# A reordered first attention stage with a contiguous mask and more filler matmuls, in a fused retention and gated MLP kernel

## The chip, the cores and the metric

The kernel runs on one core of a Trainium2 chip. The metric is the device time of one execution in microseconds (us). The time before is the median of four runs, 319.27 us (318.81 to 320.63). One of the runs was taken with the hardware profiler; its views are what this text reads.

The engines are named as in the profile: PE is the matrix engine (PEld its weight loads), DVE the vector engine, ACT the scalar engine, POOL the general-purpose engine; SP only issues DMAs here. A "q" behind a name (SPq, ACTq) is the engine's queue issuing a DMA. Each engine works through its own instructions in order and waits on semaphores for the others.

## What is computed

Eight batches, eight heads, 576 positions, head dimension 64. Attention with a decay in place of a softmax, then a gated MLP on the joined heads:

```python
scores = scale * np.matmul(q, k.transpose(0, 1, 3, 2))
gamma = 1.0 - 2.0 ** (-5.0 - np.arange(H))
Dmat = np.where(rel >= 0, gamma[:, None, None] ** rel, 0.0)   # rel = row - column
ret = np.matmul(scores * Dmat, v)                              # (B, H, S, D)
x = ret.transpose(0, 2, 1, 3).reshape(B * S, H * D)            # 4608 x 512
h = x @ w_in                                                   # 512 -> 2048
g = h * (1.0 / (1.0 + np.exp(-beta * h)))
out = g @ w_out                                                # 2048 -> 512
```

All inputs and the output are float32; the kernel works in bfloat16 with float32 accumulation.

## The kernel before

The decay is split into a gain on q (gq) and one on v (gv), so that the scores need only a 0/1 causal mask. Of each batch the first 512 positions are taken as four chunks of 128; the last 64 positions of two batches share a tail chunk. A chunk passes through these steps, each a small function:

- `pre_q`, `pre`: scale q by gq (for batch 0 on DVE), cast k to kn and scale v to vn (on POOL).
- `t_q`, `t_k` (L283, L290): transpose q and k on PE into PSUM; ACT copies the result to kT (L294), and ACT and DVE one half of qT each (L288).
- `a_sc` (L303): eight score matmuls (L311) into two PSUM tiles of 128x512, one for each half of the heads. DVE multiplies each with the mask into R (L321). The mask is one 128x128 tile, broadcast over four heads. For chunk 3 of batch 0 (`i == CB - 1`), the second PSUM tile is first copied by ACT to an SBUF tile, `half` (L318).
- `a_st` (L369): four matmuls of kn and vn (L379) that add this chunk to a running state; ACT copies it out twice, 64 partitions each (L384), to `sbd` or, for the last chunk, `end`.
- `a_cross` (L323): four matmuls of the state before this chunk with qT (L340). Chunk 0 has none.
- `a_O` (L345 to 367): eight matmuls of R and vn (L354); the sum is copied to xT, the MLP's input, by ACT (L367), and for chunk 3 by DVE and ACT, one half each (L364, L365).

The MLP of a block of 512 rows is `up` (L389: sixteen hidden blocks of four 512-column matmuls each, L396, and a Silu on ACT, L398) and `down` (L402: L409, a copy by DVE, a store issued by SP). Weights come as float32 pieces: w_in in two pieces of 256 columns and three of 512, w_out in four. They are cast by `cast_w_in` (L174) and `cast_w_out` (L186). In `cast_w_in` the first two pieces go mostly to POOL: of piece 0 only `ko == 0` is DVE's.

The order of the work is written out by hand. The first stage, batch 0's attention, is the list of calls at L440 to L477. From L484 on, batch n's MLP on PE is the "fill", and the steps of later batches (transposes, scores, state, outputs, loads) are merged into it at given positions. Loads are issued by SP in program order: q of batch 0, k and v of its four chunks, five pieces of w_in, then w_out's four, q of batch 1, k and v of its chunks, q of batch 2 and so on. Several wait until a staging buffer is free.

`warm_up(n, cols)` (L198) issues n float32 matmuls on zeros, whose result nobody reads. Here they are called filler. The profile shows each as two instructions. `betas_safe` (L209) makes four small DVE operations on the 2048 betas; Silu and the w_out casts read what it leaves.

Of the kernel before, what the change touches and what calls it, by code (L numbers as in the profile page):

```python
# [12 lines left out]
BF16 = mybir.dt.bfloat16  # L13
ACT = mybir.ActivationFunctionType
ALU = mybir.AluOpType
# [4 lines left out]
def kernel(  # L20
# [10 lines left out]
    nc = tc.nc  # L31
# [4 lines left out]
    P = 128  # L36
    HP = H // 2
# [3 lines left out]
    CB = MB // P  # L41
# [16 lines left out]
    consts = ctx.enter_context(tc.tile_pool(name="consts", bufs=1))  # L58
# [67 lines left out]
    for h in range(H):  # L126
# [12 lines left out]
    causal = consts.tile([P, P], BF16, name="causal")  # L139
    nc.gpsimd.memset(causal[:], 1.0)  # L140
    nc.gpsimd.affine_select(out=causal[:], in_=causal[:], pattern=[[1, CB], [CB, PC]], compare_op=ALU.is_ge,
                            fill=0.0, base=0, channel_multiplier=-1)

    causal2 = consts.tile([P, P], BF16, name="causal2")

# [28 lines left out]
    def cast_w_in(g, kos=range(KO)):  # L174
        t = wts[g]
        f0, fn = pieces[g]
        for ko in kos:
            on_pool = ko == KO - 1 or g == 0 and ko > 0 or g == 1 and ko > 1
            (nc.gpsimd if on_pool else nc.vector).tensor_copy(w_in_sb[:, ko, f0:f0 + fn], t[:, ko])  # L179
# [18 lines left out]
    def warm_up(n, cols=256):  # L198
        ph = psum.tile([P, MB], F32, name="ph", tag="mm", bufs=3)
        for _ in range(n):  # L200
            nc.tensor.matmul(ph[:, :cols], warm[:, :P], warm[:, :cols], start=True, stop=True,  # L201
                             skip_group_check=True)
# [6 lines left out]
    def betas_safe():  # L209

        nc.vector.tensor_tensor(tiny[:], beta_sb[:], beta_sb[:], ALU.mult)
        nc.vector.tensor_scalar(tiny[:], tiny[:], 1e-24, 1e-12, ALU.is_lt, ALU.mult)
        nc.vector.tensor_tensor(beta_sb[:], beta_sb[:], tiny[:], ALU.add)
        nc.vector.reciprocal(rbeta_sb[:], beta_sb[:])
# [5 lines left out]
    def xt(m):  # L220
        if m not in xts:
            xts[m] = xpool.tile([P, HP, CB, P], BF16, name="xT", tag="xT" if m < B else "xTt", bufs=3 if m < B else 1)
        return xts[m]
# [4 lines left out]
    def gains(g, c):  # L228
        return g[:, c, :].unsqueeze(2).to_broadcast([P, H, D])
# [15 lines left out]
    def pre(i):  # L245

        b, c = seq[i]
        vn = sb.tile([P, H, D], BF16, name="vn", tag="vn", bufs=5)
        if b is None:
            t = tail_tiles.pop(c)  # L250
            qk = sb.tile([P, 2, H, D], BF16, name="kn", tag="kn", bufs=3)
            qkT = sb.tile([P, 2, HP, P], BF16, name="kT", tag="kT", bufs=3)
            nc.gpsimd.tensor_tensor(qk[:, 0], t[:, 0], gains(gq, CB), ALU.mult)
            nc.gpsimd.tensor_copy(qk[:, 1], t[:, 1])
            nc.gpsimd.tensor_tensor(vn[:], t[:, 2], gains(gv, CB), ALU.mult)
            live[i] = dict(qk=qk, qkT=qkT, kT=qkT[:, 1], vn=vn)
            return
        if c % 2 == 0:
            pair[b, c // 2] = (sb.tile([P, 2, H, D], BF16, name="kn", tag="kn", bufs=3),
                               sb.tile([P, 2, HP, P], BF16, name="kT", tag="kT", bufs=3))  # L260
        t = kv_tiles.pop(i)
        kn, kT = pair[b, c // 2]
        live[i] = dict(kn=kn[:, c % 2], kT=kT[:, c % 2], vn=vn)
        nc.gpsimd.tensor_copy(kn[:, c % 2], t[:, 0])  # L264
        nc.gpsimd.tensor_tensor(vn[:], t[:, 1], gains(gv, c), ALU.mult)  # L265

    def heads(t, p):
        return t[:, 2 * p:2 * p + 2, :].rearrange("p h d -> p (h d)")
# [14 lines left out]
    def t_q(b, u):  # L283
        T = psum.tile([P, CB, 2, P], BF16, name="T", tag="T" if u == 0 else "mm", bufs=1 if u == 0 else 3)
        for i in range(CB):
            for p in range(2):
                nc.tensor.transpose(T[:, i, p, :], heads(batch[b]["qs"][:, i], 2 * u + p), ident[:])
        (nc.vector.tensor_copy if u else nc.scalar.copy)(batch[b]["qT"][:, :, 2 * u:2 * u + 2], T[:])  # L288

    def t_k(i):  # L290
        T = psum.tile([P, HP, P], BF16, name="T", tag="T", bufs=1)
        for p in range(HP):
            nc.tensor.transpose(T[:, p, :], heads(live[i]["kn"], p), ident[:])  # L293
        nc.scalar.copy(live[i]["kT"], T[:])  # L294

    def q_cols(i, r, p):

        b, c = seq[i]
        if b is None:
            return live[i]["qkT"][r, 0, p, :], lambda o: o  # L300
        return (batch[b]["qT"][r, :, p, c * PC:(c + 1) * PC], lambda o: o.rearrange("k (i s) -> k i s", i=CB))

    def a_sc(i):  # L303
        L = live[i]
        L["R"] = R = sb.tile([P, 2, HP, P], BF16, name="R", tag="R", bufs=2)
        sc = [psum.tile([P, HP, P], F32, name="sc", tag="sc", bufs=2) for _ in range(2)]
        for p in range(HP):
            for j in range(2):
                r = slice(j * D, (j + 1) * D)
                rhs, view = q_cols(i, r, p)  # L310
                nc.tensor.matmul(view(sc[j][:, p, :]), L["kT"][r, p, :], rhs, start=True, stop=True,  # L311
                                 skip_group_check=True)
        mask = causal if seq[i][0] is not None else causal2
        m_b = mask[:].unsqueeze(1).to_broadcast([P, HP, P])
        if i == CB - 1:

            half = sb.tile([P, HP, P], BF16, name="half", tag="half", bufs=1)
            nc.scalar.copy(half[:], sc[1][:])  # L318
            sc[1] = half
        for j in range(2):  # L320
            nc.vector.tensor_tensor(R[:, j], sc[j][:], m_b, ALU.mult)  # L321

    def a_cross(i, first):  # L323

# [18 lines left out]
    def a_O(i):  # L343

        b, c = seq[i]  # L345
        L = live[i]

        early = i < E
        if not early:
            L["O"] = psum.tile([P, HP, P], F32, name="O", tag="O", bufs=1)  # L350
        O, R, vn = L["O"], L["R"], L["vn"]
        crossed = b is None or c > 0
        for j, p in [(n // HP, n % HP) if early else (n % 2, n // 2) for n in range(H)]:
            nc.tensor.matmul(O[j * D:(j + 1) * D, p, :], vn[:, 2 * p + j, :], R[:, j, p, :],  # L354
                             start=p == 0 and not (early and crossed), stop=early or not crossed,
                             skip_group_check=True)
        if not early:
            a_cross(i, False)
        if b is None:
            x = xt(B)[:, :, c, :]  # L360
        else:
            x, O = xt(b)[:, :, :, c * PC:(c + 1) * PC], O.rearrange("k p (i s) -> k p i s", i=CB)
        if i == CB - 1:
            nc.vector.tensor_copy(x[:, :2], O[:, :2])  # L364
            nc.scalar.copy(x[:, 2:], O[:, 2:])  # L365
        else:
            (nc.scalar.copy if i < E else nc.vector.tensor_copy)(x, O[:])  # L367

    def a_st(i):  # L369

        b, c = seq[i]
        if b is None:
            return
        L = live[i]
        if c == 0:
            state_ps[b] = psum.tile([P, HP, P], F32, name="st", tag="st", bufs=1)
        st = state_ps[b]
        for p in range(HP):
            nc.tensor.matmul(st[:, p, :], heads(L["kn"], p), heads(L["vn"], p),  # L379
                             start=(c == 0 and p == 0), stop=True, skip_group_check=True)  # L380
        s = ends[b % 4] if c == CB - 1 else sbds[c % NS]
        for j in range(2):
            r = slice(j * D, (j + 1) * D)
            nc.scalar.copy(s[r, :, j * D:(j + 1) * D], st[r, :, j * D:(j + 1) * D])  # L384
# [57 lines left out]
    for n in range(4):  # L442
        pre_q(0, n)
    t_q(0, 0)
    t_q(0, 1)
    pre(0)
    t_k(0)
    a_sc(0)
    betas_safe()
    a_st(0)  # L450
    pre(1)
    t_k(1)
# [1 line left out]
    a_cross(0, True)  # L454
    a_O(0)
    a_sc(1)
    pre(2)
    a_cross(1, True)
    t_k(2)
    a_st(1)  # L460
    a_sc(2)
    pre(3)
    a_O(1)
    warm_up(1, 128)
    a_cross(2, True)
    t_k(3)
    a_st(2)
    cast_w_in(0, range(1, KO))
    a_sc(3)
    a_O(2)  # L470
    a_cross(3, True)
    a_st(3)
    warm_up(1, 128)
    cast_w_in(0, range(1))
    warm_up(1, 128)
    a_O(3)
    cast_w_in(1)  # L477

# [107 lines left out]
```

## Time and profile before

| what | value |
|---|---|
| median of four runs | 319.27 us (318.81 to 320.63) |
| the profiled execution, device time | 319.38 us |
| its span in the profile | 317.6 us |
| PE busy | 304.8 us (96%) |
| PEld / DVE / ACT / POOL busy | 155.2 / 109.0 / 142.1 / 96.7 us |
| mean granted PE clock | 0.988 of full |
| DMA moved, over the span | 52.79 MB, mean 166 GB/s |
| PE idle, longest single wait after 20 us | 1.64 us, for kT at 78.58 us |

So 1.8 us of the device time lie around the span. Row 2 of the profile page cuts the span in 40 slices of 7.9 us and gives busy tenths for each engine, the PE clock that was granted, and the DMA engines' share; one slice stands out in the clock, the second, at 5 tenths. A busy PE is no proof that PE is the bound in a stage, so the views by window, the timeline and the chain of waits are read as well. In the timeline a line has start, length, engine, source line, operation, output and inputs, shapes and count; brackets give the idle time just before and who ended it.

### The profile page before, as it was taken

What the parts mean: (1) busy time and instruction counts of PE and PEld (TensorE: products, weight loads), DVE (VectorE), ACT (ScalarE), POOL (GpSimd) and SP (SyncE); (2) the same over time, 40 slices, a digit from 0 to 9 for tenths busy, and PEclk for the clock granted to TensorE, in tenths of its full rate; (3) what the DMA queues carried; (4) which work ended last, traced back from release to release, by engine and by line L of the source; (5) the groups of instructions that cost most, each with busy time, mean ns of one, the idle gap of its engine ahead of it and who ended that gap; (6) DMA issues with size and microseconds to landing.
All of it is one profiled execution on the core that took longest, in us unless ns stands there. A gap on an engine that the chain in (4) does not pass through costs nothing.

```text
span 317.6 us, 5273 instructions
## 1 busy us (share of the span) xinstructions
PE 304.8 (96%) x2111; PEld 155.2 (49%) x2147; DVE 109.0 (34%) x193; ACT 142.1 (45%) x246; POOL 96.7 (30%) x127
## 2 busy tenths in 40 slices
PE   7889999997999999999999999999999999999994
PEld 5554455644554445444445444444454444444444
DVE  6655474123560235223323443233333320010012
ACT  5477636873228600770167215730474028207600
POOL 2752075928401932084362300833300000000000
PEclk9599999999999999999999999999999999999999
DMA  7999999999939994999999617997701110031011
GB/s 201 222 372 386 376 224 271 229 279 190 203 100 217 193 203 126 206 196 212 225 251 165 132 68 217 200 188 193 166 0 35 66 68 0 12 88 35 0 66 68
DMA packets 123368, 52.79 MB, mean 166 GB/s; under 512 B 105664, under 2 KB 115280, under 8 KB 123344
## 3 DMA queue, kind: packets, MB, share of 16 engines
q1 hardware_dynamic: 97968, 46.15, 60.6%
q10 hardware_dynamic: 25376, 6.30, 12.6%
q8 instruction: 17, 0.28, 0.4%
q14 instruction: 7, 0.06, 0.1%
HBM read 36.71 MB, written 9.44 MB: 145 GB/s over the span
## 4 chain that ended last, share of the span: by engine, by line
PE 73%; SPq 11%; DMA 8%; POOL 2%; issue 2%; DVE 1%; ACT 0%; ACTq 0%; POOLq 0%
PE po L409 33%; PE ph L396 30%; SPq L92 8%; DMA qn<-in_q_dram 4%; DMA wt<-in_moe_w_in_dram 4%; PE O L354 3%; PE sc L311 3%; PE O L340 2%; PE st L379 2%; POOL qs L241 2%; SPq L81 2%; SPq L171 1%; SPq L419 1%; DVE w_in_sb L179 0%; PE O L337 0%
## 5 line engine op out<-in xcount | busy, mean ns | idle before, releaser
L396 PE MATMUL ph<-xT,w_in_sb 128*128 128x512 bf16 (+2 forms) x575 | 127.6, 373 | 2.1 <-DVE xT L364 0.5
L409 PE MATMUL po<-w_out_sb,gT 128*128 128x512 bf16 (+2 forms) x589 | 126.8, 367 | 0.9
L398 ACT ACTIVATE gT<-ph,beta_sb 128x512 bf16<-128x512 f32 (+2 forms) x148 | 99.1, 676 | 62.7 <-PE ph L396 56.5
L396 PEld LDWEIGHTS <-w_in_sb 128*128 128x128 bf16 x592 | 56.1, 98 | 64.8 <-issue 0.9
L409 PEld LDWEIGHTS <-gT 128*128 128x128 bf16 x608 | 57.2, 98 | 61.4 <-ACT gT L398 0.3
L321 DVE TENSOR_TENSOR R<-sc,causal 128x512 bf16<-128x512 f32 x71 | 45.6, 683 | 68.7 <-PE sc L311 68.7
L416 DVE COPY ot<-po 128x512 f32<-128x512 f32 (+2 forms) x38 | 25.2, 663 | 113.8 <-PE po L409 111.2
L241 POOL TENSOR_TENSOR qs<-qn,gq 128x512 bf16<-128x512 f32 x26 | 27.5, 1082 | 64.6 <-DMA qn<-in_q_dram 64.6
L265 POOL TENSOR_TENSOR vn<-kvn,gv 128x512 bf16<-128x512 f32 x32 | 33.4, 1044 | 26.6 <-PE st L379 13.2
L384 ACT CAST sbd<-st 64x256 bf16<-64x256 f32 x48 | 17.6, 366 | 41.7 <-PE st L379 31.0
L264 POOL CAST kn<-kvn 128x512 bf16<-128x512 f32 x32 | 19.6, 611 | 28.4 <-DMA kT<-kn 11.5
L384 ACT CAST end<-st 64x256 bf16<-64x256 f32 x16 | 5.9, 366 | 37.4 <-PE st L379 37.4
L367 DVE CAST xT<-O 128x512 bf16<-128x512 f32 x28 | 19.1, 680 | 0.9 <-PE O L337 0.9
L311 PEld LDWEIGHTS <-kT 64*128 64x128 bf16 x288 | 8.5, 97 | 16.7 <-issue 11.0
L311 PE MATMUL sc<-qT,kT 64*128 64x128 bf16 x256 | 13.5, 226 | 3.2 <-ACT kT L294 3.0
L354 PE MATMUL O<-R,vn 128*64 128x128 bf16 x288 | 15.4, 230 | 0.0
L379 PE MATMUL st<-vn,kn 128*128 128x128 bf16 x128 | 12.9, 225 | 0.1
L354 PEld LDWEIGHTS <-vn 128*64 128x64 bf16 x288 | 9.5, 112 | 4.3 <-issue 0.8
L340 PE MATMUL O<-qT,sbd 128*128 128x128 bf16 x96 | 9.7, 225 | 0.0
L379 PEld LDWEIGHTS <-kn 128*128 128x128 bf16 x128 | 8.8, 100 | 1.6 <-issue 0.2
L294 ACT COPY kT<-T 128x512 bf16<-128x512 bf16 x12 | 7.0, 586 | 4.5 <-PE T L293 3.7
L201 PE MATMUL ph<-warm 128*128 128x256 f32 (+1 forms) x18 | 6.6, 516 | 1.3 <-DVE warm L114 1.3
(55 smaller groups left out, 86.3 us busy)
## 6 DMA issues: line engine op xcount, KB each, us to landing
qn<-in_q_dram SPq DMA_DIRECT2D x16, 512.0 KB, 5.7
kvn<-in_k_dram SPq DMA_DIRECT2D x32, 256.0 KB, 5.5
kvn<-in_v_dram SPq DMA_DIRECT2D x32, 256.0 KB, 5.5
out_dram<-ot SPq DMA_DIRECT2D x31, 256.0 KB, 2.8
wt<-in_moe_w_out_dram SPq DMA_DIRECT2D x4, 1024.0 KB, 9.2
wt<-in_moe_w_in_dram SPq DMA_DIRECT2D x3, 1024.0 KB, 11.0
out_dram<-ot SPq DMA_DIRECT2D x9, 128.0 KB, 2.4
wt<-in_moe_w_in_dram SPq DMA_DIRECT2D x2, 512.0 KB, 5.4
```

The lines of the kernel that those rows point to most:

```text
L92: nc.sync.dma_start(t[:, j], src[b, :, c * P:(c + 1) * P, :].rearrange("h s d -> s h d"))
L241: e.tensor_tensor(batch[b]["qs"][:, cs, hs], q_tiles[b][:, hs, cs].rearrange("p h i d -> p i h d"), gq[:, cs, hs].unsqueeze(3).to_broadcas ...
L265: nc.gpsimd.tensor_tensor(vn[:], t[:, 1], gains(gv, c), ALU.mult)
L311: nc.tensor.matmul(view(sc[j][:, p, :]), L["kT"][r, p, :], rhs, start=True, stop=True, skip_group_check=True)
L321: nc.vector.tensor_tensor(R[:, j], sc[j][:], m_b, ALU.mult)
L354: nc.tensor.matmul(O[j * D:(j + 1) * D, p, :], vn[:, 2 * p + j, :], R[:, j, p, :], start=p == 0 and not (early and crossed), stop=early or ...
L379: nc.tensor.matmul(st[:, p, :], heads(L["kn"], p), heads(L["vn"], p), start=(c == 0 and p == 0), stop=True, skip_group_check=True)
L384: nc.scalar.copy(s[r, :, j * D:(j + 1) * D], st[r, :, j * D:(j + 1) * D])
L396: nc.tensor.matmul(ph, w_in_sb[:, ko, fo * P:(fo + 1) * P], xts[m][:, ko, :, w], start=(ko == 0), stop=(ko == KO - 1))
L398: nc.scalar.activation(gts[m][:, fo, :, w], ph, ACT.Silu, scale=beta_sb[:, fo:fo + 1])
L409: nc.tensor.matmul(po[:, :nn], gT[:, fo, ms, :], w_out_sb[:, fo, n0:n0 + nn], start=(fo == 0), stop=(fo == FO - 1))
L416: nc.vector.tensor_copy(ot, po[:, :nn])
```

## The change

Five things are edited, all in the first stage:

1. A second mask tile, `causal4`, 128 x 4 x 128, is made on POOL by a copy of the mask with a broadcast; the two maskings of chunk 3 of batch 0 read it instead of the broadcast view.
2. `t_k(3)` goes from behind `a_cross(2)` to ahead of `a_O(1)`; `a_sc(3)` from behind the casts of w_in's piece 0 to ahead of them.
3. `betas_safe()` goes from behind `a_sc(0)` to behind `a_sc(1)`.
4. Filler calls of 128 columns: one more between the two q transposes, two more ahead of `a_sc(0)`, one fewer behind `a_O(1)`.
5. The two single fillers on either side of the last cast of piece 0 become one call of two ahead of it.

```diff
+    causal4 = consts.tile([P, HP, P], BF16, name="causal4")
+    nc.gpsimd.tensor_copy(causal4[:], causal[:].unsqueeze(1).to_broadcast([P, HP, P]))
...
-            nc.vector.tensor_tensor(R[:, j], sc[j][:], m_b, ALU.mult)
+            nc.vector.tensor_tensor(R[:, j], sc[j][:], causal4[:] if i == CB - 1 else m_b, ALU.mult)
...
     t_q(0, 0)
+    warm_up(1, 128)
     t_q(0, 1)
     pre(0)
     t_k(0)
+    warm_up(2, 128)
     a_sc(0)
-    betas_safe()
     a_st(0)
     pre(1)
     t_k(1)
...
     a_O(0)
     a_sc(1)
+    betas_safe()
     pre(2)
     a_cross(1, True)
     t_k(2)
     a_st(1)
     a_sc(2)
     pre(3)
+    t_k(3)
     a_O(1)
-    warm_up(1, 128)
     a_cross(2, True)
-    t_k(3)
     a_st(2)
+    a_sc(3)
     cast_w_in(0, range(1, KO))
-    a_sc(3)
     a_O(2)
     a_cross(3, True)
     a_st(3)
-    warm_up(1, 128)
+    warm_up(2, 128)
     cast_w_in(0, range(1))
-    warm_up(1, 128)
     a_O(3)
     cast_w_in(1)
```

## The prediction

> **What bounds the kernel now.** The change touches only the first stage (batch 0's attention, up to about 20 us of a span of 317.6 us), so the question is what the rest of the kernel waits for. I read three views: the windows (one row per stretch: start:end, length, busy time of PE, PEld, DVE, ACT, POOL with instruction counts, granted PE clock, DMA share, GB/s), the timeline, and the chain of waits.
>
> The first stage, one row per microsecond:
>
> ```profile
> 8.00:9.00 1.00, 0.77 (x8) 0.45 (x8) 0.51 (x2) 0.03 (x1) 0.57 (x1) 1.00 1.37 214
> 9.00:10.00 1.00, 0.32 (x7) 0.30 (x8) 0.24 (x1) 0.59 (x1) 0.72 (x1) 0.68 1.37 218
> ...
> 15.00:16.00 1.00, 1.00 (x16) 0.68 (x16) 0.42 (x1) 0.51 (x2) 0.67 (x2) 0.50 1.13 267
> 16.00:17.00 1.00, 1.00 (x17) 0.94 (x14) 0.87 (x2) 0.59 (x1) 0.66 (x1) 0.91 1.04 336
> ```
>
> The granted clock drops to 0.50 at about 9.3 us and returns to 1.00 at about 16.1, the only dip before the last slices. All the while the DMA share stays at or above 1: loads are back to back.
>
> Next, the seam between the stage and the batch-0 up-projection, in the timeline:
>
> ```profile
> 20.41 3.84 PE L396 MATMUL ph<-xT,w_in_sb 128*128 128x512 bf16 x16 [0.54 <-DVE xT L364]
> 23.20 1.51 DVE L179 CAST w_in_sb<-wt 128x512 bf16<-128x512 f32 x3 [2.36 <-DMA wt<-in_moe_w_in_dram]
> 24.43 0.10 PEld L396 LDWEIGHTS <-w_in_sb 128*128 128x128 bf16 x1 [0.65 <-DVE w_in_sb L179]
> 24.77 0.76 PEld L396 LDWEIGHTS <-w_in_sb 128*128 128x128 bf16 x5 [0.24 <-DVE w_in_sb L179]
> ```
>
> PE starts the up-projection at 20.41 us, does the four hidden blocks of w_in's first 512 columns, and then stands at the second 512. They are cast by DVE from 23.20 on; DVE had been idle 2.36 us, waiting for their DMA. Weight loads at 24.43 and 24.77 wait for those casts. This is **gate 1**: whatever PE has done before, the second load can't go before 24.4, nor the third before 24.8. After it PE runs without a gap to 34.7.
>
> Then the chain that ended last, in order of time (start, length, who):
>
> ```profile
> 15.46 13.14 DMA wt<-in_moe_w_in_dram
> 28.62 1.52 DVE w_in_sb L179 x3
> ...
> 48.90 5.76 DMA qn<-in_q_dram
> ...
> 64.63 7.56 DMA qn<-in_q_dram
> ...
> 77.94 0.59 ACT kT L294
> 78.58 0.40 PE sc L311 x8
> ```
>
> PE enters this chain only at 78.58 us. Before that it is loads, SP's issues of them, and POOL's scaling of what landed. The timeline shows the end of this stretch:
>
> ```profile
> 72.35 4.05 POOL L241 TENSOR_TENSOR qs<-qn,gq 128x512 bf16<-128x512 f32 x4 [4.72 <-DMA qn<-in_q_dram]
> 76.43 1.47 ACTq L271 DMA_TRANSPOSE qT<-qs  x1
> 77.94 0.59 ACT L294 COPY kT<-T 128x512 bf16<-128x512 bf16 x1 [0.80 <-issue]
> 78.58 0.23 PEld L311 LDWEIGHTS <-kT 64*128 64x128 bf16 x8 [1.94 <-ACT kT L294]
> 78.58 0.40 PE L311 MATMUL sc<-qT,kT 64*128 64x128 bf16 x8 [1.64 <-ACT kT L294]
> ```
>
> The q load lands at 72.35, POOL scales until 76.40, ACT's transpose DMA stands in front of its kT copy, and PE sits idle for 1.64 us. This is **gate 2**. The first stage can move the end only by getting through both.
>
> **The change part by part.** The compiled queues show which moves are real. SP's order is the same, so no load moves. PE gets two more 128-column filler calls in all; the transpose of chunk 3 (t_k(3)) goes ahead of a_O(1) and of the cross matmuls of chunk 2; DVE's four beta operations go from ahead of chunk 1's masking to behind it; ACT's kT copy of chunk 3 goes ahead of its xT copy of chunk 1; POOL gets one copy. Moving a_sc(3) ahead of the casts changes no queue's order: those casts are POOL's.
>
> *Fillers.* Two calls follow each other at 18.85 and 19.13: 0.28 us each at full clock. The new one between t_q(0,0) and t_q(0,1) lies where PE is idle 0.53 us for qs at 7.51: free. The two ahead of a_sc(0) take 2 x 0.28 = 0.56 where PE is idle 0.68 us for kT at 9.71: free at full clock. Without that cover, at the half clock, they take 1.12 and make a_sc(0) 0.44 late. The one taken out behind a_O(1) saves up to 0.37 (16.05 to 16.42). The last two are only put together: 0.
>
> Will the clock stay up? The dip begins after a stretch from 6 to 9.3 us in which PE's row is busy about two thirds; 0.84 us more makes it about nine tenths. Every matmul between 9.7 and 16.1 is paid double (eight score matmuls 0.61 against 0.40), so if the clock holds, PE has up to half of those 6.4 us, 3.2, more room there. I take it at even odds. [...]
>
> *Chunk 3's scores.* kn of chunk 3 is ready at 15.80 (POOL 15.19 + 0.61, held by its load); today t_k(3) starts at 16.65. Moved up, it starts at about 15.86, and PE now waits there for POOL. Behind this wait stand a_O(1), chunk 2's cross, a_st(2) and a_sc(3); of these ACT's xT copy of chunk 1 pays, since ACT has to do it after kT instead of before. ACT then goes: kT from about 16.25, 0.59; xT, 0.59; the two state copies, 0.76; half from about 18.1, 0.59, to 18.7. Today half ends at 18.92. So chunk 3's last R is ready 0.2 to 0.3 us earlier, and so is the up-projection: about 20.1 instead of 20.41. Bounds: if ACT's queue did not hold half, the whole 0.8 of t_k(3) and the filler would come through, about 1.0 earlier; with the clock still falling and 0.44 late at a_sc(0), 0.4 later. I take 0.3 earlier, nearest to ACT's rows.
>
> *Betas.* The four operations run from 11.62 to 13.71 and hold chunk 1's masking until 13.62, while its scores were done at about 13.3: 0.3 us off that wait. What is late next is chunk 2's masking: betas from about 13.7 take 0.9 if POOL is not in the way and 2.0 as now. The 1.04 of the first, on 16 columns, lies beside a POOL vn of 11.59 to 12.63, and the next vn is at 14.02 to 15.06. So it begins between 14.9 and 15.7, against 15.58: between 0.7 earlier and 0.1 later, with a_O(2) behind it, not the last thing late. I take 0. Their readers are far off (ACT's first at 21.48).
>
> *Mask.* The copy on POOL, 128x512, is like the kn casts, 0.61; POOL is idle 4.94 us until 7.96: free. Bounds for it: 0.3 (the select of 128 columns) to 1.1 (a two-input 512). If it held DVE's memsets (to 4.40), there are 0.83 us before DVE's next. The gain: the R from half took 0.43 with the broadcast mask, the one from PSUM 0.69. [...] By the rows alone the gain lies between 0 and 2 x 0.26 (as if both fell by the step between them); I take 0, as R from half is already at the lower row.
>
> **The sum.** Stage one: 0.3 earlier (bounds 1.0 or, with the mask's upper bound, 1.5 earlier; 0.4 later). At gate 1 all of "earlier" is lost: PE waits at w_in's second piece instead, and "later" is free up to 0.6 us: the fifth block's third matmul can't start before its load is done (24.77 + 0.10 = 24.87), and PE on its own would reach it after 18 matmuls of 0.214 (10.27 us from 24.44 to 34.71, less the 0.2 of that wait, over 47), at 20.41 + 3.85 = 24.26. Left: 0. Gate 2 would take another 1.64. So 319.38 us for the profiled execution stays 319.4; its median over runs is 319.27, 0.1 lower, so I predict **319.3 us**. Runs spread from 318.81 to 320.63; about half of that, 0.9, is what I allow for on either side.
>
> **Rivals.**
> 1. *No change, with the clock still dipping* (the fillers do not do what they are for). PE at 11 to 16 us stays doubled, the stage ends up to 0.4 late, inside gate 1's 0.6. 319.3 again. For it: PE's idle time there is mostly replaced, not removed. Together with my forecast, 0.91.
> 2. *The dip falls later, on the up-projection: slower.* A faster first stage waits more for the same loads; if the clock then falls at about 20 us and takes as long as today's 6.8 us to return, PE loses 3.4 us. Less gate 1's 0.6 that is 2.8; less gate 2's 1.64, 1.2 us: 320.5. If the delay reaches POOL and SP as well and gate 2 moves with it, the whole 2.8: 322.1. It decides from a loss of 2.2 us on (0.6 + 1.64). Against it: the up-projection's PE row is dense from 20.4. 0.05.
> 3. *The gates are softer than they look: faster.* If the w_in pieces landed earlier and gate 2 followed, the 1.0 to 1.5 us would show: 317.8 to 318.3, at most with a little of the 1.64 too, 317. Against it: DMA share 1.04 from 20 to 40 us, and an unchanged SP queue. 0.04.
>
> **How the numbers follow.** 0.5% (1.6 us) is about what a measurement of this kernel can tell from no change. Faster by more than that: 0.03, a part of rival 3. Slower: 0.04, a part of rival 2. Same: 0.93. The range takes in the forecast, rival 1 and the spread between runs, and the start of rivals 2 and 3: 318.4 to 320.3.
>
> **What would show it.** In the profile after: the clock's row at 9 to 16 us, held or not; the first up matmul between 19.0 and 20.8; DVE's casts of w_in at 23.2 as now, with a longer PE wait for them at 24.4; the score matmuls of gate 2 still at about 78.6 behind kT, idle about 1.6. I am wrong if those two times move, or if a clock dip appears after 20 us.

## The result, and the profile after

The changed kernel takes 318.89 us (median of 53 runs, 317.58 to 321.65); beside it the kernel before took 319.38 (median of 79, 317.79 to 322.97). The ratio is 0.9988, with a 95% interval of 0.9976 to 1.0000: 0.12% less, and an interval that reaches up to no change: no change by the bound of the prediction. The profiled execution took 318.56 us, its span is 316.8; before, 319.38 and 317.6. Of the 0.8 us between the spans only 0.05 are work: DVE's last copy of an output begins at 313.51 instead of 313.56. The rest lies in how long the last stores took: from the start of that copy to the end of the span 4.0 us before, 3.3 after.

So the stage did change, and the end did not. The windows of the changed kernel (columns as before):

```profile
8.00:9.00 1.00, 0.72 (x9) 0.55 (x10) 0.51 (x2) 0.07 (x1) 0.62 (x1) 1.00 1.35 217
9.00:10.00 1.00, 0.82 (x14) 0.60 (x12) 0.28 (x1) 0.59 (x1) 0.70 (x1) 1.00 1.36 221
...
15.00:16.00 1.00, 0.11 (x2) 0.11 (x3) 0.93 (x4) 0.14 (x1) 0.69 (x2) 1.00 1.13 268
16.00:17.00 1.00, 1.00 (x20) 0.81 (x19) 0.74 (x2) 0.67 (x2) 0.65 (x1) 1.00 1.09 351
```

The granted clock, third from the right, stays at 1.00. PE's busy share from 15 to 16 us falls from 1.00 to 0.11: the matmuls at a clock of 0.50 are gone, and what they leave is idle time.

The timeline of the changed kernel, at gate 1 and then at gate 2 (source lines are two higher than before):

```profile
20.15 3.98 PE L398 MATMUL ph<-xT,w_in_sb 128*128 128x512 bf16 x16 [0.52 <-DVE xT L366]
23.27 1.51 DVE L181 CAST w_in_sb<-wt 128x512 bf16<-128x512 f32 x3 [2.70 <-DMA wt<-in_moe_w_in_dram]
24.49 0.10 PEld L398 LDWEIGHTS <-w_in_sb 128*128 128x128 bf16 x1 [0.65 <-DVE w_in_sb L181]
24.83 1.19 PEld L398 LDWEIGHTS <-w_in_sb 128*128 128x128 bf16 x7 [0.24 <-DVE w_in_sb L181]
...
72.45 4.05 POOL L243 TENSOR_TENSOR qs<-qn,gq 128x512 bf16<-128x512 f32 x4 [5.06 <-DMA qn<-in_q_dram]
76.53 1.33 ACTq L273 DMA_TRANSPOSE qT<-qs  x1
77.89 0.59 ACT L296 COPY kT<-T 128x512 bf16<-128x512 bf16 x1 [0.66 <-issue]
78.53 0.40 PE L313 MATMUL sc<-qT,kT 64*128 64x128 bf16 x8 [1.50 <-ACT kT L296]
```

The up-projection starts at 20.15 us instead of 20.41. The casts it then waits for start at 23.27, 0.07 later than before, and the loads of weights behind them at 24.49 and 24.83, 0.06 later. The 0.26 us are gone at gate 1. Gate 2 is where it was.

The chain of waits of the changed kernel is the old one, piece by piece:

```profile
15.50 13.17 DMA wt<-in_moe_w_in_dram
28.70 1.52 DVE w_in_sb L181 x3
...
48.98 5.97 DMA qn<-in_q_dram
...
64.73 7.56 DMA qn<-in_q_dram
...
77.89 0.59 ACT kT L296
78.53 0.40 PE sc L313 x8
```

### The profile page after: what moved, and what is told of

Read it like the earlier page. It is cut to its first block, busy times and chain, and to the rows that moved or that the text cites. A ratio compares the mean times of both kernels' runs of the same rounds, so it can differ in the third digit from the quotient of the medians.

```text
span 316.8 us, 5283 instructions
## 1 busy us (share of the span) xinstructions
PE 302.7 (96%) x2115; PEld 153.8 (49%) x2151; DVE 108.4 (34%) x193; ACT 141.9 (45%) x246; POOL 97.0 (31%) x128
## 4 chain that ended last, share of the span: by engine, by line
PE 74%; SPq 11%; DMA 8%; POOL 3%; issue 2%; DVE 1%; ACT 0%; ACTq 0%; POOLq 0%
PE po L411 34%; PE ph L398 30%; SPq L92 8%; DMA qn<-in_q_dram 4%; DMA wt<-in_moe_w_in_dram 4%; PE O L356 3%; PE sc L313 3%; POOL qs L243 2%; PE O L342 2%; PE st L381 2%; SPq L81 2%; SPq L173 1%; SPq L421 1%; DVE w_in_sb L181 0%; PE O L339 0%
## 5 line engine op out<-in xcount | busy, mean ns | idle before, releaser
L266 POOL CAST kn<-kvn 128x512 bf16<-128x512 f32 x32 | 19.6, 612 | 27.6 <-DMA kT<-kn 11.3
L203 PE MATMUL ph<-warm 128*128 128x128 f32 (+1 forms) x22 | 6.1, 416 | 1.3 <-DVE warm L114 1.3
```

## The experiments

All ratios are to the kernel before, run on the same chip in the same job, with 95% intervals. The kernel before read medians of 319.5, 320.6 and 319.9 us in the three jobs, so kernels of different jobs are compared by ratio.

### The fillers alone, and the moved steps alone

The first kernel is the one before with edits 4 and 5, the second with edits 2 and 3.

```diff
 fillers alone
     t_q(0, 0)
+    warm_up(1, 128)
     t_q(0, 1)
...
     t_k(0)
+    warm_up(2, 128)
     a_sc(0)
...
     a_O(1)
-    warm_up(1, 128)
...
-    warm_up(1, 128)
+    warm_up(2, 128)
     cast_w_in(0, range(1))
-    warm_up(1, 128)
```

> The kernel before with the fillers of the change alone (edits 4 and 5). Theory of the two gates: the clock holds at 1.00 from 9 to 16 us as in the changed kernel, since the fillers are what holds it; the up-projection's first matmul starts at 20.2 to 20.6 us (t_k(3) is still behind the cross matmuls); PE waits for w_in's second 512 columns until 24.4 to 24.9 and for kT until 78.5; the time is within 0.3 us of both kernels, ratio 0.998 to 1.001. Rival, the clock is held by the new order and not by the fillers: a dip to 0.5 between 9 and 16 us remains. Rival, the stage passes through to the end: the time moves by as much as the first up matmul.

> The kernel before with the moved steps alone (edits 2 and 3: t_k(3), a_sc(3), the betas), its old fillers and the old mask. Theory of the two gates: the dip to 0.5 between 9 and 16 us is there as before; chunk 3's half is ready 0.1 to 0.4 us earlier than in the kernel before (18.9) because ACT's queue holds it; first up matmul 20.1 to 20.5 us; the waits at 24.4 to 24.9 and 78.5 stay; ratio 0.998 to 1.002. Rival, the order is what gains the 0.1 per cent that was measured: ratio like the changed kernel's, 0.9988, and no part of it in the fillers alone.

Measured: fillers alone 0.9987 (0.9947 to 1.0027), median 318.93; moved steps alone 1.0001 (0.9971 to 1.0032), median 319.2. The timeline of the fillers alone:

```profile
15.82 0.40 PE L293 MATMUL T<-ident,kn 128*128 128x128 bf16 x4 [0.26 <-POOL kn L264]
...
17.52 0.59 ACT L318 CAST half<-sc 128x512 bf16<-128x512 f32 x1
19.59 3.63 PE L396 MATMUL ph<-xT,w_in_sb 128*128 128x512 bf16 x16 [0.54 <-DVE xT L364]
23.05 1.51 DVE L179 CAST w_in_sb<-wt 128x512 bf16<-128x512 f32 x3 [2.83 <-DMA wt<-in_moe_w_in_dram]
24.29 2.45 PE L396 MATMUL ph<-xT,w_in_sb 128*128 128x512 bf16 x10 [0.36 <-DVE w_in_sb L179]
...
78.64 0.40 PE L311 MATMUL sc<-qT,kT 64*128 64x128 bf16 x8 [1.58 <-ACT kT L294]
```

The loads differ a little between executions, so starts are best told from DVE's first cast of w_in's third piece. By that the up-projection starts 2.79 us ahead of the cast in the kernel before (20.41 against 23.20), 3.12 in the changed one and 3.46 with the fillers alone. So the fillers bring 0.67 and the moved steps take 0.34 back. With a full clock, t_k(3) needs no move: here, behind a_O(1) and the cross matmuls, it starts at 15.82 anyhow, because POOL's kn is what it waits for. And in its old place it leaves ACT time for chunk 1's xT copy (at 15.29) before kT (16.25), so that half starts at 17.52 and not at 18.07. My expectation for the start, 20.2 to 20.6, was too late by this.

The moved steps without the fillers, windows and then timeline:

```profile
12.00:16.00 4.00, 3.44 (x39) 2.45 (x39) 2.58 (x6) 2.13 (x5) 2.86 (x4) 0.50 1.31 228
16.00:20.00 4.00, 4.00 (x42) 3.01 (x41) 1.93 (x4) 2.43 (x6) 2.63 (x6) 0.50 1.09 369
```

```profile
21.82 4.92 PE L396 MATMUL ph<-xT,w_in_sb 128*128 128x512 bf16 x22 [0.54 <-DVE xT L364]
...
78.55 0.40 PE L311 MATMUL sc<-qT,kT 64*128 64x128 bf16 x8 [0.65 <-ACT kT L294]
```

Here the dip lasts from about 9.8 until 20.0 us and the stage ends 1.4 us later than before, outside of what I expected (20.1 to 20.5). Gate 1 takes a part, gate 2 the rest: its idle time shrinks from 1.64 to 0.65, and the score matmuls start at 78.55. How much of the 1.4 is the order's and how much the longer dip's, this execution can't tell.

The mean clock of each execution shows which edit shortens the dip. The kernel before stood below 0.990 in 60 of 70 executions (median 0.984), the moved steps alone in 9 of 10, the changed kernel in 5 of 54, the fillers alone in none of 10. But the changed kernel does not hold the clock throughout: 32 of its 54 executions stand at 0.993 to 0.995, and only 17 at 0.998 or more; of the fillers alone it is 3 and 7 of 10. Three profiles further on show a dip to 0.50 of 3.4 us each, and where it can lie; 3.4 us at 0.50 make about 0.995 of a span of 317 us.

### Lateness put in on purpose

Five and twelve more filler matmuls of 256 columns ahead of the up-projection of the changed kernel:

```diff
     a_O(3)
+    warm_up(5)          # the other kernel: warm_up(12)
     cast_w_in(1)
```

> The changed kernel with five more filler matmuls of 256 columns (0.43 us each, 2.1 us) between a_O(3) and the up-projection. Two gates: the first up matmul starts 1.6 us later (21.7; 0.5 us of the filler lies in the wait for xT); gate 1 takes 0.9 of it, so PE is 0.7 to 0.8 us late from 25 us on; gate 2 takes the rest: the score matmuls stay at 78.5 with an idle time of 0.7 to 0.8 instead of 1.5 before them; time within 0.3 us of the changed kernel, ratio to the kernel before 0.998 to 1.001. Rival, no gates: 1.6 us longer, ratio 1.004. Rival, gate 1 alone: 0.75 us longer, ratio 1.001 to 1.002, and the score matmuls at 79.3.

> The changed kernel with twelve more filler matmuls of 256 columns (5.1 us) at the same place. Two gates: first up matmul at 24.7, 4.6 us late; less 0.9 at gate 1 leaves 3.7; less 1.5 at gate 2 leaves 2.2 us at the end if the loads keep their times: 321.1, ratio 1.006 to 1.008, and no idle time before the score matmuls at 78 to 81 us. If the delay reaches POOL and SP as well, so that gate 2 moves with it (the price of rival 2): 3.7 us, ratio 1.010 to 1.012. Rival, no gates: 4.6 us, ratio 1.013.

Measured: 0.9974 (0.9948 to 1.0000), median 318.7, and 1.0062 (1.0042 to 1.0081), median 320.82. The timeline of the first, then of the second:

```profile
22.09 4.70 PE L398 MATMUL ph<-xT,w_in_sb 128*128 128x512 bf16 x21
...
79.03 0.40 PE L313 MATMUL sc<-qT,kT 64*128 64x128 bf16 x8 [0.89 <-ACT kT L296]
```

```profile
24.85 1.89 PE L398 MATMUL ph<-xT,w_in_sb 128*128 128x512 bf16 x8
...
80.84 0.40 PE L313 MATMUL sc<-qT,kT 64*128 64x128 bf16 x8
```

1.9 us of lateness (1.4 against this execution's loads: 1.71 us ahead of the cast at 23.80, and not 3.12) cost nothing: both waits of gate 1 have gone (no bracket behind 22.09's matmuls), and gate 2 still has 0.89 of its 1.50 left. (The score matmuls stand 0.5 later only because this execution's loads did: its casts of w_in begin at 23.80.) With 4.7 us both gates are used up, no bracket stands at 80.84, and the last copy moves from 313.51 to 315.81: 2.3 us, where 2.2 was worked out from the two gates. No gate, or one alone, gives neither number. The delay reached POOL's scaling of q by 0.6 us only (it starts at 73.04 instead of 72.45, released by DVE's R and not by the load), less than PE was late, so it did not drag gate 2 along.

### Opening the gates

Gate 2: the kT copies of batch 2's chunks go to DVE, out of ACT's queue. Gate 1: w_in's third piece is loaded and cast in two halves.

```diff
-        nc.scalar.copy(live[i]["kT"], T[:])
+        (nc.vector.tensor_copy if i >= E else nc.scalar.copy)(live[i]["kT"], T[:])
```

```diff
-    pieces = [(0, 256), (256, 256)] + [(f, 512) for f in range(512, d_ff, 512)]
+    pieces = [(f, 256) for f in range(0, 1024, 256)] + [(f, 512) for f in range(1024, d_ff, 512)]
...
-    streams = [[(0, F(load_w_out, 0)), (2.1, F(cast_w_in, 2)), (2.2, F(load_w_out, 1)),
-                (6.1, F(cast_w_in, 3)), (6.2, F(load_w_out, 2)), (10.1, F(cast_w_in, 4)), (10.2, F(load_w_out, 3))],
+    streams = [[(0, F(load_w_out, 0)), (1.1, F(cast_w_in, 2)), (2.1, F(cast_w_in, 3)), (2.2, F(load_w_out, 1)),
+                (6.1, F(cast_w_in, 4)), (6.2, F(load_w_out, 2)), (10.1, F(cast_w_in, 5)), (10.2, F(load_w_out, 3))],
```

> The changed kernel with one line more: the kT copies of chunks after batch 1's first tail (i >= E, batch 2) go to DVE instead of ACT, so that they no longer stand behind ACT's transpose DMAs. Two gates: the score matmuls of gate 2 start at 76.9 to 77.2 us instead of 78.5, PE's wait for kT there shrinks from 1.5 to 0 to 0.4, and the end comes 1.1 to 1.5 us earlier: ratio to the kernel before 0.994 to 0.996. Rival, gate 2 is POOL or the load itself and not ACT's queue (what PE does next needs the scaled q or state as well): PE waits at the next step instead, 0 to 0.3 us gained, ratio 0.998 to 0.999.

> The changed kernel with w_in's third piece loaded and cast in two halves of 256 columns, so that the first half lands about 1.3 us earlier (gate 1 opened for the fifth and sixth hidden block). Two gates: PE's waits at 24.4 to 24.9 go, PE is 0.5 to 0.9 us earlier from 25 us on, and the wait at gate 2 grows from 1.5 to 2.0 to 2.4: the end stays, ratio to the kernel before 0.998 to 1.000, the changed kernel's. Rival, gate 1 alone decides: 0.5 to 0.9 us earlier at the end, ratio 0.996 to 0.997.

> Both edits together: gate 1 opened by the two halves, gate 2 by the kT copies on DVE. Two gates: the gains add only here: 1.1 to 1.5 us from gate 2 and 0.5 to 0.9 from gate 1, so 1.6 to 2.4 us earlier, ratio to the kernel before 0.991 to 0.994. If a third wait lies close behind gate 2 (the state copies or POOL's kn): no more than with the kT copies alone, 0.994 to 0.996.

Measured: kT on DVE 0.9922 (0.9890 to 0.9954), median 317.41; the split alone 0.9986 (0.9953 to 1.0018), median 319.44; both 0.9903 (0.9884 to 0.9923), median 317.2. Both versions with kT on DVE beat the kernel before and the changed one. The timeline of kT on DVE:

```profile
19.88 3.94 PE L398 MATMUL ph<-xT,w_in_sb 128*128 128x512 bf16 x16 [0.52 <-DVE xT L366]
...
75.08 0.42 DVE L296 COPY kT<-T 128x512 bf16<-128x512 bf16 x1 [0.81 <-PE T L295]
76.69 0.40 PE L313 MATMUL sc<-qT,kT 64*128 64x128 bf16 x8
...
311.67 0.29 DVE L418 COPY ot<-po 128x128 f32<-128x128 f32 x1 [0.60 <-PE po L411]
```

The wait at gate 2 is gone and the last copy begins 1.84 us earlier than in the changed kernel (311.67 against 313.51). 0.32 of this is the loads' (the casts of w_in begin at 22.95 and not 23.27), which leaves gate 2's 1.5. The median gained more, 0.8%, than the 0.4 to 0.6% that I expected. So gate 2 is ACT's queue, in which the kT copy (77.89 in the changed kernel) stood behind a transpose DMA (issued at 76.53) that waits for the rest of the scaled q (POOL until 76.50). PE itself does not need that transpose: here it is issued at 76.25, and the score matmuls go at 76.69 without a wait. The chain of waits no longer touches a load from 60 us on; it is PE's own work.

The split alone opens gate 1 (no wait between 20 and 27 us) and moves nothing at the end: rival "gate 1 alone" wanted 0.996 to 0.997. But gate 2 is not what took the gain: its wait is 1.49 us, and not the 2.0 to 2.4 that I expected. PE starts the first `down` 0.71 us earlier than in the changed kernel (34.06 against 34.77), and loses it in batch 1's attention, the last of it where the transposes of k wait for POOL's cast (the split, then the changed kernel):

```profile
46.65 0.40 PE L295 MATMUL T<-ident,kn 128*128 128x128 bf16 x4 [0.21 <-POOL kn L266]
...
46.67 0.40 PE L295 MATMUL T<-ident,kn 128*128 128x128 bf16 x4
```

So for work that comes early there is a third gate between the two.

The split's profiled execution has a span of 318.7 us and shows something else that I had not looked for. Its windows, then its timeline, behind gate 2:

```profile
78.00:79.00 1.00, 0.14 (x6) 0.14 (x8) 0.20 (x1) 0.58 (x1) 1.00 (x3) 1.00 1.23 228
79.00:80.00 1.00, 1.00 (x24) 0.80 (x21) 0.71 (x2) 0.00 (x0) 0.95 (x1) 0.95 1.35 236
80.00:81.00 1.00, 1.00 (x6) 0.45 (x4) 1.00 (x2) 0.00 (x0) 0.61 (x1) 0.50 1.39 190
...
83.00:84.00 1.00, 0.95 (x7) 0.57 (x7) 0.00 (x0) 0.18 (x1) 0.00 (x0) 0.84 1.28 287
```

```profile
78.86 0.40 PE L313 MATMUL sc<-qT,kT 64*128 64x128 bf16 x8 [1.49 <-ACT kT L296]
...
80.06 3.51 PE L411 MATMUL po<-w_out_sb,gT 128*128 128x512 bf16 x8
```

After the wait at gate 2 the clock falls to 0.50 from about 79.9 to 83.3 us, and eight matmuls that take 1.89 us elsewhere (the kernel with five fillers, at 80.17 and a clock of 1.00) take 3.51. From here on PE is the bound, so this 1.6 us reaches the end (last copy at 315.52, 2.0 later than in the changed kernel; 0.3 of that stood at gate 2 already). Four other profiles have a wait of 1.50 to 1.64 us in the same place (the kernel before, the changed one, the fillers alone, the mask alone) and keep 1.00 behind it. So the dip follows in some executions only. Such dips would also explain why opening gate 2 gained more than its 1.5 us in the medians.

### Fillers in gate 2's wait

To test that, three filler matmuls go into the wait itself; they shorten nothing.

```diff
+            if i == E + 2:
+                st += [(at - 0.01, F(warm_up, 3))]
             st += [(at, F(a_sc, i))]
```

> The changed kernel with three filler matmuls of 256 columns (1.3 us) in front of chunk 2 of batch 2's scores, in PE's idle time at gate 2. They take no time off the wait. Theory that the idle time of 1.5 us lets the clock fall in part of the executions (as the profile of the kernel with the split piece shows at 80 to 83 us): the slow executions go, none or one in ten above 320 us where the changed kernel has a quarter, median 0.3 to 0.8 us below the changed kernel's 318.9, ratio 0.995 to 0.998. Rival, the scatter comes from the loads or from elsewhere: the same scatter and ratio as the changed kernel, 0.9988.

Measured: 0.9957 (0.9936 to 0.9978), median 318.64, and none of 12 executions above 320 us (highest 319.48). Of the kernel before, 30 of the 70 executions with a clock on record were above 320, of the changed one 13 of 54, of the split alone 4 of 12; of the kernel with five fillers, whose wait was 0.89 us, none of 10. The timeline of its gate 2, with a clock of 1.00 around it:

```profile
77.56 1.46 PE L203 MATMUL ph<-warm 128*128 128x256 f32 x6
79.33 0.40 PE L313 MATMUL sc<-qT,kT 64*128 64x128 bf16 x8 [0.31 <-ACT kT L296]
```

The executions above 320 us are gone, as expected of a dip that the wait sets off. The dip itself was seen in one profile; that every execution above 320 us has it is inferred. The mean clocks agree with it: of the changed kernel's 13 executions above 320 us 12 stand at 0.993 to 0.995, but only 1 of its 17 at 0.998 or more is above; with the fillers alone the 3 above 320 us stand at 0.993 and 0.994, the 7 others at 0.998 or more.

Still, 5 of the 12 executions with gate 2 filled stand at 0.993 to 0.995, the profiled one among them. Its dip lies in the first stage:

```profile
12.00:16.00 4.00, 1.95 (x34) 1.28 (x32) 3.26 (x7) 1.91 (x5) 2.89 (x4) 1.00 1.30 235
16.00:20.00 4.00, 4.00 (x47) 3.24 (x46) 2.20 (x5) 3.29 (x8) 2.50 (x6) 0.59 1.05 357
```

```profile
21.27 7.08 PE L398 MATMUL ph<-xT,w_in_sb 128*128 128x512 bf16 x31 [0.54 <-DVE xT L366]
```

The clock stands at 0.50 from 16.7 to 20.1 us, behind PE's wait of 0.92 us for chunk 3's kn, and the up-projection starts at 21.27. (The profiles of the changed kernel and of the two late ones have that wait too, 0.94 us, and keep 1.00.) The profile of both gates opened has the same (0.50 from 16.2 to 19.6, a mean of 0.84 from 9 to 20 us, start at 20.99). So with the moved steps a dip can come later in the first stage than in the kernel before, and half as long (3.4 us and not 6.8). None of those five executions is above 319.11 us: in front of the gates such a dip shows no cost.

### What the first stage is worth when gate 2 is open

The kernel before with kT on DVE (the same one-line edit), and both gates opened on the kernel with the fillers alone:

> The kernel before with the kT copies of batch 2 on DVE: gate 2 is opened, the first stage is the old one. Theory (gate 2 hid most of the first stage's differences, and its idle time let the clock fall in some executions): no PE wait for kT at 76 to 79 us, the end 1.5 to 3 us earlier than the kernel before, ratio 0.991 to 0.996; but the old stage's long clock dips, which come late enough to pass gate 1, now reach the end, so it is 0.3 to 1.0 us slower than the changed kernel with the same edit (0.9922), ratio 0.994 to 0.997. Rival, the first stage is worth nothing even then, since gate 1 takes it all: the same ratio as the changed kernel with that edit, 0.992.

> The kernel before with the fillers alone (no moved steps, no second mask), w_in's third piece in two halves and the kT copies of batch 2 on DVE: both gates open, and the stage order that let the up-projection start earliest. Theory: the moved steps cost 0.3 to 0.5 us under a full clock, and with both gates open this shows at the end: 0.2 to 0.5 us below the changed kernel with the same two edits (317.2, 0.9903), ratio 0.988 to 0.9905. Rival, gate 1's next pieces (w_in at 26 and 28.7 us) take it: the same 0.990.

Measured: the old stage with gate 2 open 0.9948 (0.9926 to 0.9970), median 318.66; the fillers alone with both gates open 0.9932 (0.9907 to 0.9957), median 317.39. The timeline of the old stage with gate 2 open:

```profile
22.14 10.10 PE L396 MATMUL ph<-xT,w_in_sb 128*128 128x512 bf16 x45 [0.54 <-DVE xT L364]
...
78.12 0.40 PE L311 MATMUL sc<-qT,kT 64*128 64x128 bf16 x8
...
313.10 0.29 DVE L416 COPY ot<-po 128x128 f32<-128x128 f32 x1 [0.60 <-PE po L409]
```

Its clock dip runs from 11.2 until about 21.5 us (its window from 20 to 24 us has a mean clock of 0.82), the up-projection starts 2.26 us later than in the changed kernel with the same edit (22.14 against 19.88), gate 1 takes 0.8 of it, the score matmuls are 1.43 later (78.12 against 76.69), and so is the last copy (313.10 against 311.67): once gate 2 is open, all that passes gate 1 reaches the end. In these two profiles, whose loads are alike (casts at 22.98 and 22.95), the change is worth 1.43 us; with gate 2 shut it was 0.05. The ratios point the same way (0.9948 against 0.9922), but were taken in different jobs and their intervals overlap.

The last one is a miss. I expected the better stage order to show, with 0.988 to 0.9905. Its timeline:

```profile
27.33 6.98 PE L396 MATMUL ph<-xT,w_in_sb 128*128 128x512 bf16 x30 [0.36 <-DVE w_in_sb L179]
...
46.81 0.40 PE L293 MATMUL T<-ident,kn 128*128 128x128 bf16 x4 [0.18 <-POOL kn L264]
```

PE starts the up-projection at 19.48, 1.51 us earlier than in the changed kernel with both gates open, whose profiled stage had the dip told above. But it waits at 27.33 for w_in's next piece, which leaves 0.67 of this at the first `down` (34.14 against 34.81), and in batch 1's attention the rest goes: these transposes of k start at 46.81 against 46.82, and the last copy of both begins at 312.04. So the next piece of w_in is the next gate, as the rival there said, and batch 1's kn, as with the split alone, the one behind it.

### The mask alone

```diff
+    causal4 = consts.tile([P, HP, P], BF16, name="causal4")
+    nc.gpsimd.tensor_copy(causal4[:], causal[:].unsqueeze(1).to_broadcast([P, HP, P]))
...
+            nc.vector.tensor_tensor(R[:, j], sc[j][:], causal4[:] if i == CB - 1 else m_b, ALU.mult)
```

> The kernel before with the contiguous mask alone (edit 1). Prediction's step: the R from half takes 0.43 us as with the broadcast mask, the R from PSUM 0.69, the stage and the time stay. Rival, the copied mask makes either faster (0.3 or 0.5 us) or the longer 0.51 us that the changed kernel shows for R from half comes from the mask itself and not from POOL's casts beside it: then 0.5 here too.

One run: 319.39 us. Its timeline:

```profile
18.80 0.69 DVE L323 TENSOR_TENSOR R<-sc,causal 128x512 bf16<-128x512 f32 x1 [2.21 <-POOL w_in_sb L181]
19.41 0.64 DVE L323 TENSOR_TENSOR R<-half,causal 128x512 bf16<-128x512 bf16 x1
```

Nothing is faster. The R from PSUM stays at 0.69. The R from half takes 0.64 here, 0.51 in the changed kernel and 0.43 and 0.42 in the changed kernel with the split, without and with kT on DVE; with the broadcast mask it takes 0.43 in four profiles and 0.66 in a fifth (the fillers with both gates open). The other profiles with the second mask lie between 0.47 and 0.58. So both masks reach 0.43 and both are sometimes longer, the second one more often. What stretches it stays open; it is not on the path.

## Why the prediction was right

- **The sum, right.** 319.3 us was forecast and 318.89 measured, within the range, and no change as forecast. Gate 1 and gate 2 each took what the prediction said: the late kernels give their sizes back, 2.3 us at the end for 4.7 put in.
- **The fillers, right in part.** At even odds I took it that they hold the clock. From 9 to 16 us they do in the profiles (1.00; with the moved steps alone 0.50 from about 9.8 on), and the long dips are gone in nearly all executions (below 0.990 in 5 of 54, against 60 of 70), but 32 of the 54 have a mean clock that fits one short dip. That the row would be nine tenths busy from 6 to 9.3 us was too much: it went from 2.00 to 2.49 us of 3.3, three quarters. They cost nothing: a_sc(0) starts at 9.75 instead of 9.71. "Paid double" is read from the granted clock of 0.50; the rows show less for groups of small matmuls (eight score matmuls 0.61 us and 0.40 without the dip) and 3.51 us against 1.89 for eight of 512 columns.
- **The start of the up-projection, right by two errors.** 20.1 was forecast, 20.15 measured, and half ran at 18.07 to 18.66 as worked out. But the step "chunk 3's scores" gave the 0.3 us to the moved steps. The runs show the clock worth 0.67 and the moved steps costing 0.34: I had compared ACT's order with the kernel before at the half clock, and not with the old order at the full one.
- **The betas, right.** They ran 13.87 to 15.60, one of them again 1.03 us (from 14.07) beside POOL's vn (14.04 to 15.08), and chunk 2's masking began at 15.52.
- **The mask, right.** No gain shown: with the second mask alone the R from PSUM took 0.69 us and the R from half 0.64, against 0.69 and 0.43 in the kernel before.
- **Rival 1's "0.4 later", too small.** I read one profile of the kernel before, with a mild dip (mean clock 0.988, against a median of 0.984). With the usual longer dips the stage ends later than gate 1 can take (21.6 to 22.1 us in three profiles with the old fillers). Gate 2 took the remainder, so the forecast held, but with less to spare than it said.
- **Rival 2, right in kind, too dear.** A dip that comes later does exist. In two profiles with the whole change it fell at 16.2 to 20.1 us, just ahead of the up-projection, and lasted 3.4 us and not 6.8: at most 1.7 us lost, below the 2.2 from which the rival decides. The starts of the up-projection in them (21.27 and 20.99) lie ahead of the 22.09 that the late kernel shows to be free. The prediction had no dip behind gate 2's own wait; the one profile that shows it lost 1.6 us to it.
- **The 0.12%.** Its interval touches no change. Fewer executions above 320 us (13 of 54 against 30 of 70) go with it; no profile of either kernel caught such an execution, so the cause is open.

## What to carry to other kernels

A stage that ends earlier can be worth nothing until the next waits are opened, and behind each opened wait there may be another: find the waits behind it whose releaser does not depend on it, add up their idle times, and check them by putting lateness in. Here one line that took a copy out of a queue in which it stood behind a waiting transpose DMA was worth several times the whole rebuilt stage (0.9922 against 0.9988). And a short wait on PE is to be priced with the clock dip that can follow it: here 3.4 us at 0.50 behind 1.49 us of wait, in one of five profiles with such a wait.

## What the runs showed of the hardware

A PE wait of 1.49 us was followed by half the granted clock for 3.4 us, with the matmul row at 0.95 or more from 72 to 76 us and from 79 us on, and 41% busy between 76 and 79. Four profiles with the same wait, 1.50 to 1.64 us, show no fall. What decides between the two is not shown. With the wait filled with matmuls on zeros, none of 12 executions was above 320 us.

The first stage's dip is not one length: the mean clock of the kernel before ran from 0.979 to 0.998 over 70 executions. The seven dips that the profiles show while PE works last 3.4 us (79.9 to 83.3, 16.7 to 20.1, 16.2 to 19.6), 6.8 us (9.3 to 16.2, the kernel before) and 10.2 us (9.8 to 20.0 with the moved steps alone and with the mask alone, 11.2 to 21.5 with the old stage and gate 2 open): one, two and three times 3.4. One profile of such a stage is one draw.
